# A transformer block on one core: later row passes for block 3, and an order of its own for the first attention quad

## The chip, the cores and the metric

The kernel runs on one core of a Trainium2 chip. The metric is the device time of one execution in microseconds (us). Beside the times there is a profile of one execution, with every instruction of the engines: TensorE (PE for matmuls, PEld for weight loads), VectorE (DVE), ScalarE (ACT), GpSimd (POOL) and SyncE (SP, which issues the DMAs).

## What is computed

A block with adaptive layer norms, 2048 rows of 576 values, 32 heads of 18 channels that share one key and one value head, and an MLP with 4608 hidden channels. All values are fp32.

```
mod = silu(c) @ w_mod                         # six rows: sa, ca, ga, sb, cb, gb
h = layernorm(x) * (1 + ca) + sa
q = h @ wq;  k = h @ wk;  v = h @ wv          # 32 heads of q, one k, one v
p = softmax(q k^T * 18**-0.5)
x = x + ga * ((p v) @ wo)
h = layernorm(x) * (1 + cb) + sb
x = x + gb * (gelu(layernorm(h) @ w1 + b1) @ w2 + b2)
```

## The kernel before

**The first part: projections.** The 2048 rows are four blocks (tb = 0 to 3) of 512. For each block the normalized rows are turned (channels on partitions) into a tile zt of five chunks of channels, k = 0 to 4. Each chunk is kept as a rounded part and a remainder, so that products keep their precision. `h_evac` makes a chunk: ScalarE applies scale and shift into a buffer hf (three buffers, L249); the rounded part zt[k] is a copy of hf, by ScalarE (L253) or, where `first` is set, by VectorE (L251); the remainder zt[KD+k] is hf minus the rounded part, by the engine `e` (L254).

For blocks 1 and 2 `h_chunk` turns the rows by matmuls with an identity. Block 3's rows are turned by VectorE and two trips through memory instead: they are stored to hscr and loaded back by `h_load` (L211, L213), which is issued in block 2's second step (i = 1), and `h_chunk` takes the loaded rows.

`q_chunk` projects one chunk m of queries (and, in m = 4, keys and values): 14 matmuls (L272), three for each k up to 3 and two for k = 4, into one of three psB banks; ScalarE evacuates it twice (qf L302, qs L303), GpSimd subtracts (L304), and SP stores it to qscr. In every block the steps i = 0 to 4 take m = 4, 0, 1, 2, 3. Between a chunk's matmuls `mid` puts parts of the row maxima of the first quads: one part is two pairs of matmuls (L343), each into one of two psA tiles, and two reductions on VectorE (L368). In block 2 there is one part in each step, and two in the last one. In block 3 larger units (`smax_half`, L361) follow.

While block 2 is projected, `h_chunk` for block 3 is called in the steps i = 2 (k = 0 to 2) and i = 3 (k = 3 and 4), behind `q_chunk` of the same step. The order of the calls is the order of each engine's queue: the schedule is written by hand.

**The attention.** 32 quads of four heads by 512 rows follow. The order of work of a quad is a list of tokens: S0, S1 a score matmul on one half of the array's rows (L987, into one of four psB banks), which ScalarE turns into exponentials in P (L989); M0, M1 a matmul for a row maximum of a coming quad (L343, one of three psM banks), reduced by VectorE (L1009); X1 and R1 two steps of a shorter way to a maximum (X: L997, ScalarE L1000; R: L343, VectorE L1007); Vn the product with the values for n quarters of a chunk of 128 keys (L977), which lags eight quarters behind; F1 and F2 finish the maxima of the next quad and put them into its query tile by four DMAs (L388); the others are steps of the quad before, which do nothing in the first quad. In quad 0, each M token while 3 to 7 quarters have been counted is preceded by one matmul whose result isn't used (L1064). QUAD is the list of the quads 0 to 8, QUADW of 9 to 30, LAST of 31.

The rest (output projection, second layer norm, MLP) is not touched.

Of the kernel before, what the change touches and what calls it, by code (L numbers as in the profile page):

```python
# [15 lines left out]
NB = 4  # L16
TB = S // NB
NT = TB // 128
KD = 5
NQ = H // 4  # L20
# [12 lines left out]
def block_kernel(ctx: ExitStack, tc, x, wqkv, wo, w1, b1, w2, b2, c, wmod, ident_in, out):  # L33
    nc = tc.nc
    ve, ac, po, pe, sy = nc.vector, nc.scalar, nc.gpsimd, nc.tensor, nc.sync
# [17 lines left out]
    def psB(): return PS["t"].tile([128, 512], F32, name="psB", bufs=PS["b"])  # L53
# [3 lines left out]
    def big(): return per.tile([128, 10, 512], F32R, name="big", bufs=3)  # L57
# [99 lines left out]
    def tr(o, Z, k):  # L157
        pe.transpose(o, Z[:, 128 * k:128 * (k + 1)], ident)
# [45 lines left out]
    def h_rows(tb):  # L204

        return Zs[tb].rearrange("p t c -> p (t c)").rearrange("p (k n) -> p k n", n=TB)
# [39 lines left out]
    def h_evac(p, zt, k, e, first=False):  # L246

        hf = p1.tile([128, TB], F32, name="hf", bufs=3)
        ac.activation(hf, p, AF.Identity, scale=mcol[:, 1, k:k + 1], bias=mcol[:, 0, k:k + 1])  # L249
        if first:  # L250
            ve.tensor_copy(zt[:, k, :], hf)  # L251
        else:
            ac.activation(zt[:, k, :], hf, AF.Copy)  # L253
        e.tensor_tensor(zt[:, KD + k, :], hf, zt[:, k, :].bitcast(F32), op=ALU.subtract)  # L254

    def h_chunk(tb, zt, k):
        if tb == NB - 1:
            p = h_rows(tb)[:, k]
        else:
            p = psB()  # L260
            for t in range(NT):
                tr(p[:, 128 * t:128 * (t + 1)], Zs[tb][:, t, :], k)
        h_evac(p, zt, k, ve if tb == 1 and k in (1, 3, 4) else po, tb == 1 and k < 3)

    def proj(o, wh, wl, c0, c1, zt, mid=None, n=0):
        terms = []
# [27 lines left out]
    def q_chunk(tb, m, zt, mid, n):  # L294

        w = 126 if m < KD - 1 else 128
        wd = 126 if m < KD - 1 else 72
        pq = psB()
        proj(pq[:w], wqh, wql, 126 * m, 126 * m + w, zt, mid, n)
        qs = p1.tile([128, 2, TB], F32R, name="qs", bufs=2)  # L300
        qf = p1.tile([128, TB], F32, name="qf", bufs=2)
        ac.activation(qf[:w], pq[:w], AF.Copy)  # L302
        ac.activation(qs[:w, 0], pq[:w], AF.Copy)  # L303
        po.tensor_tensor(qs[:w, 1], qf[:w], qs[:w, 0].bitcast(F32), op=ALU.subtract)  # L304
        if m == KD - 1:
            if tb >= 2:
                key_diff(tb, qf)
        sy.dma_start(qscr[tb, :, 126 * m:126 * m + wd, :].rearrange("s p t -> p s t"), qs[:wd].bitcast(F32))
        return qf, qs

    def k_block(tb, qs):

        pk = psB()
        for i in range(2):
            pe.matmul(pk, pick[:, i, :], qs[:, i, :], start=(i == 0), stop=(i == 1))
        ac.activation(KS[:, TB * tb:TB * (tb + 1)], pk, AF.Identity, bias=ones)

    def v_block(tb, qf):
        pk = psB()
        for i in range(NT):  # L320
            pe.transpose(pk[:, 128 * i:128 * (i + 1)], qf[:, 128 * i:128 * (i + 1)], ident)
        ve.tensor_copy(V[:, NT * tb:NT * (tb + 1), :DH],
                       pk.rearrange("p (i c) -> p i c", i=NT)[:, :, 72:72 + DH])
# [80 lines left out]
    zt = big()  # L404
# [22 lines left out]
    def dense(n, w, x):  # L427

        p = psB()
        for _ in range(n):  # L430
            pe.matmul(p, w, x, start=True, stop=True)
# [36 lines left out]
    def unit():  # L468
        nonlocal u1
        smax_half(1, u1 % 2, u1 // 2)  # L470
        u1 += 1
# [5 lines left out]
    for tb in range(NB):  # L477
        nz = big() if tb + 1 < NB else None
        for i, m in enumerate((4, 0, 1, 2, 3)):
            np_ = NPART[tb][i]  # L480
            if i == 2:
                parts.extend((u, tb) for u in range(8))
            mid = {(NB - 1, 1): unit, (NB - 1, 4): lambda: last.popleft()()}.get((tb, i), part)
            qf, qs = q_chunk(tb, m, zt, mid, np_ + 1 if np_ else 0)
            if i == 0:
                qv = qf, qs
            if i == 1:
                k_block(tb, qv[1])
                v_block(tb, qv[0])
                if tb == 0:  # L490
                    load_q(0)
            if i == 2:
                if tb == 0:
                    load_q(1)
            if tb == NB - 1:
                if i == 0:
                    unit()
                elif i == 3:
                    smax_fin1(0)
                if i == 4:  # L500
                    dense(5, wqh[:, 0, :128], KS[:, :512])
                    unit()
                    dense(4, wqh[:, 0, :128], KS[:, :512])
            if nz is not None:
                if tb == NB - 2 and i == 1:
                    h_load(tb + 1)
                for k in {1 + tb // 2: (0, 1, 2), 2 + tb // 2: (3, 4)}.get(i, ()) if tb else {3: (0, 1, 2), 4: (3, 4)}.get(i, ()):
                    h_chunk(tb + 1, nz, k)
            if tb < 2:
                for _ in range(NAPPLY[tb][i]):  # L510
                    b, t = applies.popleft()
                    ln1_apply(b, t, ve if b == 1 and t % 2 else ac)
                for _ in range(NSTAT[tb][i]):
                    ln1_stats(*stats.popleft())
        zt = nz
# [262 lines left out]
    def wo_add(tb, t, h2, p):  # L778
        X = XT[:, NT * tb + t, 288 * h2:288 * (h2 + 1)]
        ve.tensor_tensor(X, p[:, :288], X, op=ALU.add)  # L780
# [143 lines left out]
    def tail_parts(o, tail, d, e=po):  # L924

        e.tensor_tensor(d, tail[:, 0], tail[:, 1], op=ALU.subtract)
        for x, y in ((o[:, :2], tail), (o[:, 2], d)):
# [11 lines left out]
    QUAD = """S0 M0 S1 S1 M0 V3 S0 M1 S1 M0 M1 S0 V3 M0 S1 M1 S0 V2 M0 S1 S1 M0 X1 S0 V4 T1 X1 M0 M1 M0 S1 S0  # L939
            V4 S1 RC M0 S1 S0 M0 S0 M1 V3 S0 M1 R1 S1 S0 M0 X1 V3 M0 S1 S1 R1 S0 M0 S1 V3 M0 X1 M0 S0 S1 S0  # L940
            M1 V3 M0 S1 S1 M0 S0 R1 S0 V3 R1 S0 S1 M1 S0 M0 X1 V3 M0 S1 M0 S1 S0 S0 R1 V3 M0 X1 S0 M1 S0 M1
            V3 S1 M0 M0 S1 T2 S0 S1 V4 M0 S1 S0 M1 S0 M1 V3 S0 R1 S1 M0 F1 S1 S0 V3 X1 M0 S1 M0 R1 S0 F2 OS
            V4 M0 M1 S0 S1 M0 X1 V4 S1 M0 S1 S0 M1 M0 S1 V2 R1 S0 M1 S0 V2 S0 S1 M0 M1 V2 S1""".split()
    QUADW = """M1 M1 S0 S0 X1 S1 M0 V4 S1 M0 S1 S0 M1 M0 V4 M0 S1 S0 M0 S1 T1 M0 X1 V4 S1 RC S0 S0 M1 M0 S1 V4
            S0 R1 M1 S0 S1 M0 S1 V3 S1 M0 S0 X1 M0 M0 S1 V2 M0 S1 S0 R1 V2 M0 X1 M0 S1 S0 S1 M0 V4 S0 T2 R1
            M0 S1 OS S0 M1 WO S0 R1 M1 S0 M1 S0 X1 V3 S0 M1 M0 S1 S1 M1 S0 V3 M0 S1 S0 R1 S0 M0 X1 V3 M0 S1
# [91 lines left out]
    for n in range(NQT):  # L1038
        ns = [0, 0]
        if n < NQT - 1:  # L1040
            order = QUADW if n > NQ else QUAD
        else:
            order = LAST
        if n < NQT - 1:
            kf, kr = (sum(int(tok[1]) for tok in order[:order.index(a)] if tok[0] == "V") // 4 for a in ("F2", "RC"))
            quiet = kf - 2, kf - 1, kr - 1
        for tok in order:
            if tok[0] == "V":
                g = int(tok[1:])
                while g:  # L1050
                    i = min(g, 4 - pq % 4)
                    if pq >= LAG:
                        pv_mm(*divmod((pq - LAG) // 4, 16), pq % 4, pq % 4 + i)
                    pq, g = pq + i, g - i
                    if pq % 4 == 0:
                        between(*divmod(pq // 4 - 1, 16))
            elif tok[0] == "S":
                g = int(tok[1])
                two = sum(ns) % 7 % 2 if n == NQT - 1 else ns[g] % 2 and n == NQT - 2 and ns[g] > 24
                st_mm(n, ns[g] // 2, g, ns[g] % 2, psM if two else psB)  # L1060
                ns[g] += 1
            elif tok in maxima:
                if n == 0 and 3 <= pq < LAG and tok[0] == "M":
                    pe.matmul(idle, KS[:64, :128], KS[:64, :512], start=True, stop=True)  # L1064
                unit = next(maxima[tok], None)
                if unit:
                    mx_mm(*unit, tok[0], int(tok[1]))
            elif tok == "WO":
                wo_next(psB)
            elif tok == "WP":  # L1070
                h2 = part.popleft()
                p = psB()
                wo_mm(NB - 1, 2, h2, p, 0, KD - 1, KD - 1)
                wo_add(NB - 1, 2, h2, p)
            elif tok == "RW":
                for i, w in enumerate("hl"):
                    sy.dma_start(WO[w][:, KD - 1, :].bitcast(F32), woscr[i])
            elif tok[0] == "F":
                (smax_fin1 if tok == "F1" else smax_fin2)(n + 1)
            elif n:  # L1080
                if next(posts[0], 0) == 0:
                    posts.pop()
        if n == NQT - 1:
            W1["r"] = per.tile([128, 40, 128], F32R, name="w1a", tag="big", bufs=3)
            load_w1(0, " ".join(OPS) + " tails")
# [482 lines left out]
```

## Time and profile before

| what | value |
|---|---|
| median of 3 runs | 2213.87 us (2212.64 to 2214.05) |
| profiled execution | 2212.6 us |
| its span, first to last instruction | 2210.3 us |
| projections (first part) | to about 128 us |
| first quad | about 128 to 166 us |

The profile's span leaves out what lies ahead of the first and behind the last instruction. Times in the rows are counted from the span's start. In a timeline a row is one or more instructions of a line (xcount) that follow one another; its first two numbers are the start and the time to the end of the last one, and in brackets stands how long the engine was idle before and what ended that.

### The profile page before, as it was taken

The page shows a single profiled execution, that of the slowest core. Times are in us where ns is not written, and L with a number is a line of the kernel's source. Part 1 is how long each engine was busy: PE and PEld are TensorE (multiplying, and loading weights), DVE is VectorE, ACT ScalarE, POOL GpSimd, SP SyncE. Part 2 cuts the span into 40 slices and gives each one's busy share as a digit, 9 for nine tenths or more (in the row PEclk, how much of TensorE's full clock was granted, in tenths as well). Part 3 has the DMA queues.
Part 4 walks back from the last instruction along what each step waited for, and adds up shares of the span by engine and source line. Part 5 has one row for each costly group of instructions (what it writes and reads, how often), then busy time and mean ns, then how long its engine had stood idle before and what let it go on. Part 6 is the DMA issues. An engine that isn't in the chain of part 4 may idle for free.

```text
span 2210.3 us, 46102 instructions
## 1 busy us (share of the span) xinstructions
PE 2189.5 (99%) x16554; PEld 1439.5 (65%) x16554; DVE 1938.3 (88%) x3425; ACT 1624.8 (74%) x3110; POOL 1521.7 (69%) x1760
## 2 busy tenths in 40 slices
PE   8999999999999999999999999999999999999999
PEld 6655444444544545444454445899898899889898
DVE  7689999999999999999999993888888878787887
ACT  5579999999999999999999998544445444343443
POOL 7654456666777678678675640888899767877776
PEclk9999999999999999999999999999999999999999
DMA  6432143433443442343343321666767746676664
GB/s 231 131 133 93 35 134 118 136 130 113 136 130 125 127 141 98 126 139 117 123 131 121 125 71 59 204 194 190 203 185 199 207 133 179 184 218 188 178 184 124
DMA packets 243688, 320.16 MB, mean 145 GB/s; under 512 B 67871, under 2 KB 133807, under 8 KB 243461
## 3 DMA queue, kind: packets, MB, share of 16 engines
q1 hardware_dynamic: 243317, 317.08, 47.0%
q8 instruction: 131, 2.15, 0.4%
q14 instruction: 96, 0.79, 0.1%
q10 hardware_dynamic: 144, 0.15, 0.0%
HBM read 207.23 MB, written 99.69 MB: 139 GB/s over the span
## 4 chain that ended last, share of the span: by engine, by line
PE 95%; DVE 2%; ACT 1%; POOL 1%; issue 1%; DMA 1%; SPq 0%; ACTq 0%; POOLq 0%; DVEq 0%
PE psC L977 24%; PE psB L1204 18%; PE psA L1307 16%; PE psB L987 14%; PE psM L343 13%; PE psB L776 2%; PE psB L997 2%; PE psA L1341 1%; PE psB L272 1%; PE psA L776 1%; PE psA L343 0%; DMA Z<-hscr 0%; DVE mx L368 0%; PE psB L381 0%; PE psM L987 0%
## 5 line engine op out<-in xcount | busy, mean ns | idle before, releaser
L989 ACT ACTIVATE P<-psB 128x512 f32<-128x512 f32 x2013 | 1054.9, 620 | 48.7 <-PE psM L343 26.9
L1009 DVE TENSOR_REDUCE mx<-psM 128x1 f32<-128x512 f32 x1476 | 931.2, 682 | 26.0 <-PE psM L343 11.0
L987 PE MATMUL psB<-qst,KS 64*128 64x512 f32 x2013 | 604.2, 433 | 0.1
L343 PE MATMUL psM<-KS,qst 64*128 64x512 f32 x1722 | 592.5, 434 | 0.4 <-DVE mx L361 0.3
L977 PE MATMUL psC<-P,V 128*32 128x256 f32 (+3 forms) x6608 | 568.1, 439 | 0.0
L987 PEld LDWEIGHTS psB<-qst,KS 64*128 64x128 f32 x2013 | 301.9, 184 | 216.2 <-ACT P L989 184.7
L343 PEld LDWEIGHTS psM<-KS,qst 64*128 64x128 f32 x1722 | 285.1, 184 | 188.4 <-DVE mx L1009 139.4
L1204 PE MATMUL psB<-ops,w1a 128*128 128x512 f32 x1512 | 393.8, 396 | 0.2 <-DVE h L1219 0.2
L1204 PEld LDWEIGHTS psB<-ops,w1a 128*128 128x128 f32 x1512 | 270.1, 188 | 46.8 <-DVE h L1219 0.6
L977 PEld LDWEIGHTS psC<-P,V 128*32 128x32 f32 x6608 | 147.0, 108 | 187.9 <-issue 160.1
L1313 DVE TENSOR_TENSOR XT<-psA,XT 128x576 f32<-128x576 f32 x330 | 241.5, 752 | 16.2 <-PE psA L1307 10.7
L1307 PEld LDWEIGHTS psA<-w2s,big 128*128 128x128 f32 x1584 | 223.7, 188 | 12.2 <-DVE XT L1313 0.2
L1307 PE MATMUL psA<-w2s,big 128*128 128x288 f32 x1584 | 230.2, 294 | 0.0
L1281 POOL TENSOR_TENSOR big<-s,big 128x512 fp32r<-128x512 f32 x132 | 171.1, 1296 | 10.6
L1007 DVE CUSTOM_DVE_ANT_0 xc<-psM,xc 128x512 f32<-128x512 f32 x246 | 165.9, 681 | 11.2 <-PE psB L987 5.7
L1217 ACT ACTIVATE psB<-gs 128x512 f32<-128x512 f32 x144 | 86.7, 602 | 120.8 <-DVE gs L1216 120.8
L1213 ACT ACTIVATE h<-psB,b1t 128x512 f32<-128x512 f32 x144 | 98.1, 681 | 105.2 <-PE psB L1204 98.7
L1000 ACT ACTIVATE xc<-psB 128x512 f32<-128x512 f32 x246 | 153.8, 625 | 3.9 <-PE psB L987 1.2
L813 POOL TENSOR_TENSOR os<-O,os 128x512 fp32r<-128x512 f32 x31 | 39.9, 1287 | 169.1 <-ACT os L812 169.1
L1216 DVE SCALAR_TENSOR_TENSOR gs<-psB,h 128x512 f32<-128x512 f32 x144 | 98.9, 687 | 38.8 <-ACT psB L1214 38.7
L847 POOL TENSOR_TENSOR r<-r,r 128x256 fp32r<-128x256 f32 (+1 forms) x162 | 122.0, 753 | 13.0
L1222 ACT ACTIVATE big<-h 128x512 fp32r<-128x512 f32 x39 | 24.7, 634 | 139.3 <-DVE h L1219 139.3
(219 smaller groups left out, 3290.4 us busy)
## 6 DMA issues: line engine op xcount, KB each, us to landing
w1a<-w1scr SPq DMA_DIRECT2D x252, 256.0 KB
w2s<-w2sum SPq DMA_DIRECT2D x132, 288.0 KB
w1scr<-r SPq DMA_DIRECT2D x126, 256.0 KB
w2s<-w2scr SPq DMA_DIRECT2D x76, 288.0 KB
w2scr<-r SPq DMA_DIRECT2D x72, 288.0 KB
w2sum<-r SPq DMA_DIRECT2D x72, 288.0 KB
qst<-qscr SPq DMA_DIRECT2D x192, 72.0 KB
w1a<-w2scr SPq DMA_DIRECT2D x33, 288.0 KB
```

The source lines that it names most:

```text
L343: pe.matmul(o, QST[n][64 * g:64 * g + 64, p, 128 * qt:128 * (qt + 1)], KS[64 * g:64 * g + 64, 512 * kb:512 * (kb + 1)], start=True, stop=True)
L847: po.tensor_tensor(o[:, n:2 * n], src, o[:, :n].bitcast(F32), op=ALU.subtract)
L977: pe.matmul(PVt[n][32 * j:32 * (j + 1), cs], V[:, kc, :], t[:, j, cs], start=(kc == 0 and h0 == 0), stop=(kc == 15), skip_group_check=True)
L987: pe.matmul(t, KS[64 * g:64 * g + 64, 128 * kc:128 * (kc + 1)], QST[n][64 * g:64 * g + 64, i, :], start=True, stop=True)
L989: ac.activation(P[n, kc][:, 2 * i + g, :], t, AF.Exp, scale=SCALE)
L1000: ac.activation(XC[-1], t, AF.Relu)
L1007: ve.tensor_tensor_reduce(c, t, c, 1.0, -3.0e38, ALU.add, ALU.max, o)
L1009: ve.tensor_reduce(o, t, axis=AX.X, op=ALU.max)
L1204: pe.matmul(o, x, y, start=(first and i == 0), stop=(i == len(terms) - 1), skip_group_check=True)
L1281: po.tensor_tensor(unit(u, 1), x, unit(u, 0).bitcast(F32), op=ALU.subtract)
L1307: pe.matmul(p[:, i, :288], x[:, ts_], W2S[k][:, y], start=(bool(first) and q == 0), stop=(q == 2), skip_group_check=True)
L1313: ve.tensor_tensor(o, p[:, :, :288], o, op=ALU.add)
```

## The change

Three edits. The remainders of block 3's chunks 1 and 3 are subtracted on VectorE instead of GpSimd, and the rounded parts of its chunks 0 to 2 are copied on VectorE instead of ScalarE. All five chunks of block 3 are made in step i = 3 of block 2, behind the projection of m = 2; before, three were made in step 2 and two in step 3. Quad 0 gets a list of its own, QUAD0, with 19 V tokens where QUAD has 21, and F1 and F2 later in the list; the counts of S, M, X and R are the same.

```diff
-        h_evac(p, zt, k, ve if tb == 1 and k in (1, 3, 4) else po, tb == 1 and k < 3)
+        on_ve = {1: (1, 3, 4), NB - 1: (1, 3)}.get(tb, ())
+        h_evac(p, zt, k, ve if k in on_ve else po, tb in (1, NB - 1) and k < 3)
...
-                for k in {1 + tb // 2: (0, 1, 2), 2 + tb // 2: (3, 4)}.get(i, ()) if tb else {3: (0, 1, 2), 4: (3, 4)}.get(i, ()):
+                for k in ({3: (0, 1, 2), 4: (3, 4)}, {1: (0, 1, 2), 2: (3, 4)}, {3: range(KD)})[tb].get(i, ()):
                     h_chunk(tb + 1, nz, k)
...
+    QUAD0 = """S1 S0 M1 S0 V4 M0 S1 M0 S1 S0 M1 V4 S1 M0 T1 M1 S0 S1 S0 M1 V4 X1 M0 R1 S0 X1 M0 S0 V3 S1 M0 S1 S0
+            M1 M0 S1 V3 M1 S0 S1 M0 X1 M0 S1 V3 M0 S1 M0 S1 S0 M1 V3 M0 S1 S0 S0 R1 M1 S0 V3 S1 M0 S0 S1 R1 S1
+            M0 V3 M0 X1 S0 S1 M1 M0 S1 V3 M1 S0 RC S0 X1 R1 M0 S1 V3 S1 M0 S0 R1 S0 M0 S1 V4 S0 M1 S0 X1 M0 X1
+            M0 V4 M0 S1 M0 R1 S0 S1 S0 V4 X1 M0 S0 R1 S1 M0 V3 M0 S1 S0 S1 M1 S0 V4 F1 M0 S1 M0 M1 S0 S1 F2 V3
+            S0 R1 S0 S1 M1 S1 M0 V3 M0 T2 S1 S1 S0 M0 OS M1 S0 V3 S0 M1 M0""".split()
...
-            order = QUADW if n > NQ else QUAD
+            order = QUADW if n > NQ else QUAD if n else QUAD0
```

For comparison, QUAD begins and ends so:

```
S0 M0 S1 S1 M0 V3 S0 M1 S1 M0 M1 S0 V3 M0 S1 M1 S0 V2 M0 S1 S1 M0 X1 S0 V4 T1 X1 M0 M1 M0 S1 S0 V4 ...
... S0 R1 S1 M0 F1 S1 S0 V3 X1 M0 S1 M0 R1 S0 F2 OS V4 M0 M1 S0 S1 M0 X1 V4 S1 M0 S1 S0 M1 M0 S1 V2
R1 S0 M1 S0 V2 S0 S1 M0 M1 V2 S1
```

## Rows read from the trace of the kernel before

**Rows 1.** The page, part 1: busy time, share of the span, instructions.
```profile
PE 2189.5 (99%) x16554; PEld 1439.5 (65%) x16554; DVE 1938.3 (88%) x3425; ACT 1624.8 (74%) x3110; POOL 1521.7 (69%) x1760
```
**Rows 2.** Windows: length, busy time by engine, granted clock, DMA.
```profile
93.00:102.90 9.90, 8.07 (x33) 4.04 (x31) 5.70 (x5) 8.77 (x16) 8.74 (x7) 1.00 0.17 56
```
**Rows 3.** Timeline of ScalarE around block 3's rows.
```profile
92.45 0.81 ACT L249 ACTIVATE hf<-Z,mcol 128x512 f32<-128x512 f32 x1 [5.27 <-DMA Z<-hscr]
...
96.58 0.58 ACT L302 ACTIVATE qf<-psB 126x512 f32<-126x512 f32 x1
```
**Rows 4.** Timeline of TensorE, block 2's last steps and block 3's first.
```profile
84.08 3.53 PE L272 MATMUL psB<-big,wA 128*126 128x512 f32 x14
...
91.18 0.73 PE L343 MATMUL psA<-KS,qst 64*128 64x512 f32 x4
...
93.19 0.50 PE L343 MATMUL psA<-KS,qst 64*128 64x512 f32 x2
94.13 0.49 PE L343 MATMUL psA<-KS,qst 64*128 64x512 f32 x2 [0.44 <-DVE mx L368]
94.55 3.13 PE L272 MATMUL psB<-big,wA 128*126 128x512 f32 x11
...
102.89 1.89 PE L272 MATMUL psB<-big,wA 128*126 128x512 f32 x7
```
**Rows 5.** Waits from 84 to 103.5 us: total, times, longest.
```profile
PE psB L272 <- POOL big L254: 1.3, 2, 1.0
...
PEld psA L343 <- ACT qs L303: 0.4, 1, 0.4
```
**Rows 6.** Timeline of VectorE in block 2's last step.
```profile
91.72 4.62 DVE L368 TENSOR_REDUCE mx<-psA 128x2 f32<-128x1024 f32 x4 [1.28 <-PE psA L343]
```
**Rows 7.** The tile hf: durations in ns (min/median/max), first and last start.
```profile
L253 ACT ACTIVATE big<-hf x14: 631/634/637, 20.3 to 99.8; 128x512 fp32r<-128x512 f32 x14
L254 POOL TENSOR_TENSOR big<-hf,big x12: 1262/1288/1301, 45.0 to 100.5; 128x512 fp32r<-128x512 f32 x12
...
L251 DVE CAST big<-hf x6: 372/424/427, 19.6 to 42.3; 128x512 fp32r<-128x512 f32 x6
L249 ACT ACTIVATE hf<-Z,mcol x5: 799/802/817, 92.4 to 98.9; 128x512 f32<-128x512 f32 x5
```
**Rows 8.** Timeline of all engines, block 1's projection.
```profile
47.75 0.69 DVE L254 TENSOR_TENSOR big<-hf,big 128x512 fp32r<-128x512 f32 x1 [3.14 <-ACT big L253]
...
47.86 0.74 PE L343 MATMUL psA<-KS,qst 64*128 64x512 f32 x4
...
49.70 1.21 DVE L368 TENSOR_REDUCE mx<-psA 128x2 f32<-128x1024 f32 x1
```
**Rows 9.** Groups by line and shape, 24 to 29 us: count, busy, mean ns.
```profile
L415 POOL TENSOR_TENSOR wA<-bigw,wA 128x504 fp32r<-128x504 f32 x2 | 3.4, 1695 | 4.5 <-issue 4.5
...
L415 DVE TENSOR_TENSOR wA<-bigw,wA 128x504 fp32r<-128x504 f32 x1 | 1.3, 1306 | 0.4 <-ACT wA L413 0.4
```
**Rows 10.** Windows near the start: busy time by engine, granted clock, DMA.
```profile
15.00:18.50 3.50, 2.89 (x29) 2.58 (x27) 2.88 (x6) 1.62 (x6) 1.98 (x3) 1.00 1.06 374
19.00:22.00 3.00, 3.00 (x15) 2.90 (x14) 2.19 (x4) 2.97 (x5) 0.65 (x2) 0.50 1.05 391
```
**Rows 11.** Window of the first quad.
```profile
128.00:166.00 38.00, 37.57 (x344) 19.14 (x345) 36.30 (x69) 35.95 (x72) 27.44 (x16) 1.00 0.42 144
```
**Rows 12.** Timeline of ScalarE, first quad's start.
```profile
128.66 5.37 ACT L989 ACTIVATE P<-psB 128x512 f32<-128x512 f32 x10 [2.46 <-PE psB L987]
```
**Rows 13.** Timeline of TensorE in the first quad.
```profile
133.63 1.07 PE L977 MATMUL psC<-P,V 128*32 128x512 f32 x8
...
138.76 0.40 PE L987 MATMUL psB<-qst,KS 64*128 64x512 f32 x1
...
139.00 0.39 PE L987 MATMUL psB<-qst,KS 64*128 64x512 f32 x1
```
**Rows 14.** Timeline of SyncE, first quad's end.
```profile
159.66 2.85 SPq L388 DMA_DIRECT2D qst<-ms  x4
```

## The prediction

> **What bounds the kernel now.** I read the page first: TensorE is busy 99% of the span [rows 1], so the kernel gains only where TensorE waits, and loses where it is made to. The change touches two places: block 3's rows in the projections (80 to 103 us) and the first attention quad (128 to 166 us). So the windows came next, then the timelines of these places engine by engine, and the waits.
>
> In the first place TensorE is busy 8.07 of 9.90 us, ScalarE and GpSimd nearly throughout [rows 2]. ScalarE stands 5.27 us until the loaded rows arrive, at 92.45, and evacuates chunk m=2 of block 2 only at 96.58, since the row passes are ahead of it in its queue [rows 3]. On TensorE the reader should find the two maxima parts of chunk m=3. Call them B (91.18) and C (93.19, its second tile at 94.13 after 0.44 us for VectorE). Then the last four matmuls of m=3 run on into block 3's chunk m=4 (94.55), and chunk m=0 begins at 102.89 [rows 4]. Within that stretch TensorE waits 1.3 us by name for GpSimd's subtractions [rows 5]. VectorE reduces B and C in one go of four from 91.72, with 1.28 us of idleness ahead [rows 6].
>
> **The row passes: what they remove and add.** Five 0.80 us passes on ScalarE stay; three of its 0.63 us roundings become VectorE copies of 0.42, and two of the five GpSimd subtractions of 1.29 [rows 7] become VectorE subtractions of 0.69 [rows 8]. All five chunks now follow m=2's evacuation. That frees m=2's PSUM bank some 6 us earlier, but little waits for it: three banks rotate, and the one wait that names ScalarE's qs is 0.4 us of a weight load [rows 5]. No DMA moves: the load is issued where it was, so the rows still arrive at 92.45; the store of m=2 goes out earlier, behind that arrival.
>
> What costs is the queue of VectorE. It gets the new copies and subtractions ahead of B's and C's reductions, because m=3 is issued after them. psA has two tiles; B fills both, so C cannot start before B is reduced. Does VectorE keep the program's order? In block 1, whose evacuation has the same mix, it sat 3.14 us for a rounding at 47.75, and only at 49.70 reduced a tile whose matmuls began at 47.86 [rows 8]: the next subtraction stands between. I take it that it does.
>
> The chain [rows 7, 8]: the first pass ends at 92.45+0.80 = 93.25; the copy takes it to 93.7; GpSimd's subtraction to 95.0. There are three hf buffers, so the fourth pass (k=3) waits for this subtraction: 95.0 to 95.85, its rounding on ScalarE to 96.5, its subtraction on VectorE to 97.2. Copies and subtraction of k=1 and 2 fit in between. Only then can B be reduced. (The fifth chunk has nothing on VectorE; its subtraction on GpSimd ends at about 99.5, ahead of its use.)
>
> Two of VectorE's subtractions now meet one on GpSimd. Near the start there is such a meeting: 1.31 us on VectorE where 0.69 is usual, and 1.70 on GpSimd where 1.29 is [rows 9]. The bounds are 0 and (1.31-0.69)+(1.70-1.29) = 1.0 us on the chain; the meetings overlap only in part, so I take 0.6, and B's reductions start at 97.8. The Trainium skill (GPSIMD Engine Reference, section Specifications) says that the two engines share their SBUF interfaces, and counts VectorE's two-port operations as well as those with two SBUF inputs. By that rule the new copies too would slow GpSimd, an estimate of 0.2 us more; no row here shows it.
>
> Each reduction takes 4.62/4 = 1.16 us [rows 6]. C's first tile can start at 97.8+1.2 = 99.0, its second at 100.2 against 94.13 now: 6.1 us late. TensorE stands from about 93.2 to 99.0, then but for two matmuls to 100.2. Part of it comes back. From 94.55 to 102.89 there are 8.34 us, in which 18 projection matmuls at 0.25 (fourteen take 3.53) and two maxima parts of about 0.7 are 5.9 us of work [rows 4]; the other 2.4 us are waits for the row passes and go, as all passes are done before. In their place the unit after m=4 waits some 0.5 us for VectorE, which is still two reductions behind. Net: 6.1-2.4+0.5 = **+4.2 us**, bounds 3.5 (no meeting) to 4.6 (full). Everything behind follows TensorE's order, so I see no slack that takes this back.
>
> **The clock.** The granted clock was 1.00 from 15.0 to 18.5, while TensorE did only small matmuls with waits between, and 0.50, its 1.2 GHz level, from 19 to 22 [rows 10]. A stand of nearly 6 us is emptier than that stretch. By the rows alone a fall is one occurrence; I give it seven in ten. Its price: at the lower level matmuls last twice as long. If the level is back up before C is through, only C's matmuls are longer, about 0.2 us. If it lasts into the dense stretch behind, 5 us of it at half rate lose 2.5. I take **1.3 us**, the middle. The Trainium skill (TensorE: Matmul & The Clock Gate, section HAM oscillation) says that waits between bursts of matmuls put the array back to its lower clock, a rule that speaks against the change. By it every run would pay, and rival (a) below would drop out.
>
> **The first quad.** It takes 38.0 us, with ScalarE busy 35.95 and VectorE 36.30 [rows 11]. The counts are the same in both orders (64 S, 48 M, 8 X, 8 R), so it can't get much below these two. The old order has 11 S, one X and 9 M before the first V that does work, which starts at 133.63 [rows 13]. Four psB tiles allow the twelfth evacuated tile only after the eighth evacuation: 128.66+8x0.53 = 132.9 [rows 12]. In the new order 10 S and 7 M stand ahead, so the tenth waits for the sixth, 131.9, and the first V comes about 1.3 us earlier. One S, one X and two M are left for later, and some stand worse for running on both row halves at once: by the tokens 62 slots behind the first V against 58, a slot being 0.24 us (138.76 to 139.00) [rows 13], so 1.0 us more. That leaves 0.3. One working V token fewer helps a little, and ScalarE and VectorE, already within 1.7 to 2.1 us of the quad's length, may bring a wait. I take **-0.3 us**, bounds -1.4 (38.0 less the 36.3, and 0.3 for the start) and +1 (two evacuations' worth of waits).
>
> The filling matmuls of the start go from 5 to 3; they stand where TensorE waits for evacuations anyway. F2 comes about 2 us nearer to the quad's end. Its four DMAs keep SP 2.85 us from 159.66 [rows 14], with a quad end near 166; two microseconds later the last is issued about 1.5 us ahead of the S that reads it, so a short wait is possible there, which the +1 covers.
>
> **Sum.** Without the clock: 4.2-0.3 = +3.9. With it: +5.2. Against the profiled execution's 2212.6 us that is 2217.8; the median of the runs shown is 1.3 us above that execution, so I forecast 2213.9+5.2 = 2219.1. A measurement of this kernel tells about 0.2%, 4.4 us, from no change; the forecast lies just beyond.
>
> **Rivals.** (a) *Held, but the clock stays up*: 2217.8, within the bound. For it: one fall is on record in this trace. Against it: TensorE never stands so long elsewhere in the projections. (b) *Not slower: VectorE reduces B as soon as it is ready*, at 91.7, ahead of the row passes. Then C starts at 94.1 as now, the copies slip in between reductions, the 1.3 us of waits go [rows 5], and with -0.3 the time is 2212.3. It decides if C's second tile starts before 95; the order in block 1 speaks against it [rows 8]. (c) *The new order of the first quad costs*: ScalarE or VectorE run dry, or F2's rows land late. At +1 instead of -0.3, on top of hold and clock: 2220.4. For it: the 1.5 us above; against it: equal counts.
>
> **Chances.** Held with the fall 0.58, (a) 0.24, (b) 0.06, (c) 0.12. Of the first some three quarters lie beyond 4.4 us (the clock's price must exceed 0.5), of (a) a fifth (full meeting, nothing from the quad), of (c) nearly three quarters: slower 0.57, within 0.40, faster 0.03, the last from (b) with more waits gone than I found. The range goes from 2214.5, which leaves (b) out, to 2221.5, hold and fall with the upper half of the clock's price and of (c).
>
> **What would show it.** Right: a gap on TensorE from about 93 to C's first tile at 98.5 to 99.5, released by VectorE's mx; on VectorE copies from 93.3 and a subtraction that ends at 97 to 98; a granted clock of 0.50 somewhere in 96 to 105; chunk m=0 of block 3 at 106.5 to 109 instead of 102.89; from ScalarE's first P to the first working V 3.7 us instead of 5.0; the first quad 0 to 1 us shorter, later quads as long as now. Wrong: rows that arrive before 90, C before 95, or a first quad above 38 us.

## The result, and the profile after

The changed kernel takes 2219.25 us (median of 8 runs, 2218.38 to 2221.19), the kernel before 2213.21 us beside it (8 runs): a ratio of 1.0028, 95% interval 1.0017 to 1.0038, or 6.0 us more. The profiled execution took 2219.56 us with a span of 2217.5 us. Of all the executions timed for this document one stands out, 5708 us for the kernel with the gap filled (below), for which the record gives no cause; the median of its eleven hardly feels it. In the changed kernel the line numbers are higher by 1 in the first part and by 6 in the attention.

TensorE's timeline, from part B of chunk m=3 to block 3's chunk m=0 (110.36):

```profile
91.79 0.73 PE L344 MATMUL psA<-KS,qst 64*128 64x512 f32 x4
...
100.08 0.79 PE L344 MATMUL psA<-KS,qst 64*128 64x512 f32 x2 [6.21 <-DVE mx L369]
101.21 0.80 PE L344 MATMUL psA<-KS,qst 64*128 64x512 f32 x2 [0.34 <-DVE mx L369]
101.94 4.88 PE L273 MATMUL psB<-big,wA 128*126 128x512 f32 x11
106.75 0.73 PE L344 MATMUL psA<-KS,qst 64*128 64x512 f32 x4
...
110.36 1.89 PE L273 MATMUL psB<-big,wA 128*126 128x512 f32 x7
```

Part B stands 0.6 us later than before [rows 4]; that is ahead of the change and not part of it (in the kernel with only the first quad's order, below, whose rows are those of before, B stands at 92.05). Counted from B, chunk m=0 came 11.71 us later before and comes 18.57 us later now: 6.9 us are lost here. The loss starts at one place, 6.21 us in which TensorE waits for VectorE's mx, where it waited 0.44 us [rows 4]. What follows is slow too: eleven matmuls take 4.88 us where they took 3.13, waits included.

VectorE's timeline over the same stretch:

```profile
93.88 0.43 DVE L251 CAST big<-hf 128x512 fp32r<-128x512 f32 x1 [2.84 <-ACT hf L249]
94.58 1.35 DVE L251 CAST big<-hf 128x512 fp32r<-128x512 f32 x1 [0.28 <-ACT hf L249]
95.97 0.69 DVE L254 TENSOR_TENSOR big<-hf,big 128x512 fp32r<-128x512 f32 x1
96.58 0.42 DVE L251 CAST big<-hf 128x512 fp32r<-128x512 f32 x1
97.20 1.69 DVE L254 TENSOR_TENSOR big<-hf,big 128x512 fp32r<-128x512 f32 x1 [0.20 <-ACT big L253]
98.81 4.60 DVE L369 TENSOR_REDUCE mx<-psA 128x2 f32<-128x1024 f32 x4
```

VectorE was idle for 2.84 us up to 93.88, the last 1.5 of them with the first tile of part B ready (about 92.3); but the copy of k=0 was next in its queue and waited for ScalarE's first pass. Two of the five row operations are long, the copy of k=1 (1.35 us, others 0.42) and the subtraction of k=3 (1.69, the other 0.69). ScalarE and GpSimd show what they met:

```profile
93.03 2.23 ACT L249 ACTIVATE hf<-Z,mcol 128x512 f32<-128x512 f32 x3 [1.15 <-DMA Z<-hscr]
95.69 0.82 ACT L249 ACTIVATE hf<-Z,mcol 128x512 f32<-128x512 f32 x1 [0.43 <-POOL big L254]
```
```profile
94.39 1.27 POOL L254 TENSOR_TENSOR big<-hf,big 128x512 fp32r<-128x512 f32 x1 [1.09 <-DVE big L251]
97.07 1.27 POOL L254 TENSOR_TENSOR big<-hf,big 128x512 fp32r<-128x512 f32 x1 [1.42 <-DVE big L251]
98.61 1.40 POOL L254 TENSOR_TENSOR big<-hf,big 128x512 fp32r<-128x512 f32 x1 [0.27 <-ACT big L253]
```

Each long operation began while a GpSimd subtraction was running (94.58 behind 94.39, 97.20 behind 97.07), and that subtraction itself kept its 1.27 us. The windows (length, busy time of PE, PEld, DVE, ACT, POOL, granted clock, DMA) show why TensorE is slow behind the gap:

```profile
93.00:96.00 3.00, 0.87 (x4) 0.38 (x2) 1.81 (x3) 2.54 (x4) 1.56 (x2) 1.00 0.57 198
96.00:98.00 2.00, 0.00 (x0) 0.00 (x0) 1.80 (x3) 1.94 (x4) 0.93 (x1) 0.56 0.01 3
98.00:100.00 2.00, 0.00 (x0) 0.00 (x0) 2.00 (x3) 0.53 (x1) 1.73 (x2) 0.50 0.00 0
...
102.00:104.00 2.00, 2.00 (x6) 1.63 (x6) 1.42 (x2) 0.00 (x0) 0.00 (x0) 0.50 0.00 0
104.00:107.00 3.00, 3.00 (x10) 2.06 (x10) 0.00 (x0) 1.08 (x2) 1.27 (x1) 0.59 0.00 0
```

The granted clock falls to 0.50 inside the gap and is back only near the end of the last window.

The first quad, after, in TensorE's and ScalarE's timelines: the first score matmul, the first working V, a broadcast that stands behind the last V (L560), and ScalarE's evacuation of the finished quad during the next one (L792).

```profile
135.35 0.50 PE L993 MATMUL psB<-qst,KS 64*128 64x512 f32 x2
...
139.65 1.06 PE L983 MATMUL psC<-P,V 128*32 128x512 f32 x8
...
171.75 0.43 PE L560 MATMUL psB<-bigw,unity 128*32 128x144 f32 x8
```
```profile
177.97 0.61 ACT L792 ACTIVATE O<-psC 128x512 f32<-128x512 f32 x1
```

The same four marks before, the first V being that of [rows 13]:

```profile
128.13 0.61 PE L987 MATMUL psB<-qst,KS 64*128 64x512 f32 x2
...
165.32 0.43 PE L559 MATMUL psB<-bigw,unity 128*32 128x144 f32 x8
```
```profile
170.95 0.61 ACT L791 ACTIVATE O<-psC 128x512 f32<-128x512 f32 x1
```

From the first score matmul they come after 5.50 (133.63), 37.19 and 42.82 us before, after 4.30, 36.40 and 42.62 us now: 1.2 us is won at the first V, 0.8 is left behind the last V, and 0.2 when the next quad evacuates.

### The profile page after: what moved, and what is told of

It is laid out like the page before. It is cut to its first block, busy times and chain, and to the rows that moved or that the text cites. A ratio compares the mean times of both kernels' runs of the same rounds, so it can differ in the third digit from the quotient of the medians.

```text
span 2217.5 us, 46084 instructions
## 1 busy us (share of the span) xinstructions
PE 2192.7 (99%) x16544; PEld 1440.8 (65%) x16544; DVE 1942.1 (88%) x3430; ACT 1622.8 (73%) x3107; POOL 1517.6 (68%) x1758
## 4 chain that ended last, share of the span: by engine, by line
PE 95%; DVE 2%; ACT 1%; POOL 1%; DMA 1%; issue 1%; SPq 0%; ACTq 0%; POOLq 0%; DVEq 0%
PE psC L983 24%; PE psB L1210 18%; PE psA L1313 16%; PE psB L993 14%; PE psM L344 13%; PE psB L777 2%; PE psB L273 2%; PE psB L1003 2%; PE psA L1347 1%; PE psA L777 1%; PE psA L344 1%; DVE mx L369 0%; DMA Z<-hscr 0%; PE psB L382 0%; PE psM L993 0%
```

## The experiments

The theory after the result: (1) VectorE, in the order of its queue, holds parts B and C behind the row operations; (2) the empty gap lets the clock fall, which costs some 2 us more; (3) the first quad's order gives something back. The rivals are named with each run. All times are medians beside runs of the kernel before on the same chip: 2213.45 us for the first four kernels, 2213.51 for the others.

**Only the rows' edit.** The first quad goes by QUAD again.

```diff
-            order = QUADW if n > NQ else QUAD if n else QUAD0
+            order = QUADW if n > NQ else QUAD
```

> Only the edit of block 3's rows; the first quad keeps its old order. Theory (the rows cost some 6.9 us, a hold of 4.5 and a clock price of 2.4, and the new first quad gives back 0.8): 2220.0 us, chunk m=0 of block 3 7 us later than before, the first quad 38 us as before. Rival (the first quad's order is worth nothing, or what it gains is lost in the next quads): 2219.2 us, the same as with both edits.

Measured: 2220.23 us, ratio 1.0030 (1.0019 to 1.0042). The whole loss is the rows'. The time is at the theory's value, but the intervals don't part it from the changed kernel; the marks of its first quad do: 37.13 us to the broadcast and 42.78 to the evacuation, as before the change.

**Only the first quad's order.** QUAD0 in the kernel before.

```diff
+    QUAD0 = """S1 S0 M1 S0 V4 M0 S1 ...""".split()
-            order = QUADW if n > NQ else QUAD
+            order = QUADW if n > NQ else QUAD if n else QUAD0
```

> Only the new order of the first quad; block 3's rows as before. Theory: 2212.4 us, 0.8 less than before (2213.2), first working V 4.3 us after the first S instead of 5.5, no wait for F2's rows. Rival (the gain is lost in the next quads): 2213.2 us; rival (the order costs when it isn't started late): 2214 us or more.

Measured: 2213.36 us, ratio 0.9999 (0.9990 to 1.0008). The interval holds the theory's 2212.4 as well as the first rival's 2213.2, so the time doesn't decide; the marks do. Here too the first V comes early (133.15 after 128.84) and the broadcast after 36.41 us, but the evacuation only after 42.64, where the kernel before has 42.82. So the theory's 0.8 us, read at the broadcast behind the last V, shrinks to 0.2 in the next quad: by the marks the rival holds.

**The gap filled.** TensorE works through most of the gap.

```diff
+    def filled_part():
+        seen.append(0)
+        if len(seen) == 2:
+            dense(24, wqh[:, 0, :128], KS[:, :512])
+        part()
...
-            mid = {(NB - 1, 1): unit, (NB - 1, 4): lambda: last.popleft()()}.get((tb, i), part)
+            mid = {(NB - 1, 1): unit, (NB - 1, 4): lambda: last.popleft()(), (2, 4): filled_part}.get((tb, i), part)
```

> The changed kernel, with 24 matmuls whose result isn't used on TensorE between the second five matmuls of m=3 and part C, so that the gap stays and TensorE works in it. Theory (the clock falls for the empty gap and costs 2.4 us): granted clock 1.00 from 94 to 107, C at the same time as in the changed kernel, 2216.8 us. Rival (the hold on VectorE is all, what runs slower on TensorE is hidden behind it): clock 1.00 but 2219.2 us.

Measured: 2217.99 us, ratio 1.0022 (1.0012 to 1.0031). The clock column of the windows stays at 1.00:

```profile
98.00:100.00 2.00, 1.57 (x7) 0.94 (x5) 2.00 (x2) 0.87 (x2) 1.75 (x2) 1.00 0.00 0
100.00:102.00 2.00, 0.91 (x4) 0.37 (x4) 2.00 (x3) 0.00 (x0) 0.40 (x1) 1.00 0.00 0
102.00:104.00 2.00, 2.00 (x11) 1.63 (x10) 1.80 (x2) 0.74 (x2) 0.00 (x0) 1.00 0.00 0
```
```profile
91.89 0.73 PE L344 MATMUL psA<-KS,qst 64*128 64x512 f32 x4
...
93.82 5.75 PE L432 MATMUL psB<-KS,wA 128*128 128x512 f32 x24
100.46 0.50 PE L344 MATMUL psA<-KS,qst 64*128 64x512 f32 x2 [0.90 <-DVE mx L369]
101.60 0.50 PE L344 MATMUL psA<-KS,qst 64*128 64x512 f32 x2 [0.63 <-DVE mx L369]
102.02 2.82 PE L273 MATMUL psB<-big,wA 128*126 128x512 f32 x11
...
108.39 1.89 PE L273 MATMUL psB<-big,wA 128*126 128x512 f32 x7
```
```profile
93.36 2.23 ACT L249 ACTIVATE hf<-Z,mcol 128x512 f32<-128x512 f32 x3 [1.37 <-DMA Z<-hscr]
```

The reader is to see that C still waits for VectorE, at the same place, while the eleven matmuls behind it take 2.82 us instead of 4.88. From C's second tile to m=0 are 6.79 us here (101.60 to 108.39) and 9.15 in the changed kernel (101.21 to 110.36). So the lower clock costs 2.36 us by the rows, 2.05 behind the start of the eleven matmuls and 0.3 in C's second tile; the theory had 2.4. By the medians it is 1.5 us (4.5 above the kernel before, against 6.0), and 2.2 beside the kernel with only the rows' edit, timed in the same round. The interval of this run holds the theory's time as well as the rival's, so it is the rows that decide.

What is left, the hold alone, is 4.5 us: 6.9 lost between B and m=0 in the changed kernel, less 2.36. Counted in this run itself it is 16.50-11.71 = 4.8, but here C came 0.3 us later behind B (8.57 us after it, 8.29 in the changed kernel), mostly because the loaded rows did: the first pass starts 1.47 us behind B, 1.24 in the changed kernel. Over the runs in which the passes wait for the rows and B has its old place this arrival lies 1.0 to 1.7 us behind B, and the hold goes with it, so one profile gives the hold to some tenths of a us.

**No row operation on VectorE.** The move to the later step stays.

```diff
-        on_ve = {1: (1, 3, 4), NB - 1: (1, 3)}.get(tb, ())
-        h_evac(p, zt, k, ve if k in on_ve else po, tb in (1, NB - 1) and k < 3)
+        on_ve = {1: (1, 3, 4)}.get(tb, ())
+        h_evac(p, zt, k, ve if k in on_ve else po, tb == 1 and k < 3)
```

> The changed kernel with block 3's copies on ScalarE and all its subtractions on GpSimd again: only the move to the later step and the first quad's order are left. Theory (the copies and subtractions on VectorE hold part C): no gap, C's second tile at about 94.1 to 94.7, TensorE waits at most 1.3 us for the last subtractions, clock 1.00, 2211.4 to 2212.4 us. Rival (passes made one step later are late for chunk m=4, whichever engine makes them): TensorE waits 3 us or more at m=4, 2215 us or more.

Measured: 2211.63 us, ratio 0.9991 (0.9982 to 1.0000), as the theory had it and below the rival's time.

```profile
94.30 0.49 PE L344 MATMUL psA<-KS,qst 64*128 64x512 f32 x2 [0.44 <-DVE mx L369]
94.72 2.84 PE L273 MATMUL psB<-big,wA 128*126 128x512 f32 x11
...
99.33 0.97 PE L273 MATMUL psB<-big,wA 128*128 128x512 f32 x3 [0.21 <-POOL big L254]
100.69 0.49 PE L273 MATMUL psB<-big,wA 128*128 128x512 f32 x1 [0.40 <-POOL big L254]
...
101.78 1.89 PE L273 MATMUL psB<-big,wA 128*126 128x512 f32 x7
```

C starts as in the kernel before, and TensorE's named waits for GpSimd shrink from 1.3 us [rows 5] to 0.6. From B (91.34) to m=0 are 10.44 us, 1.3 less than before, so by the rows the move to the later step is good by itself. This is the fastest kernel of the study, 1.8 us under the kernel before, and its interval just reaches no change; beside the kernel with only the first quad's order, which it differs from by the move alone, it is 1.7 us faster.

**The subtraction of k=3 on GpSimd.**

```diff
-        on_ve = {1: (1, 3, 4), NB - 1: (1, 3)}.get(tb, ())
+        on_ve = {1: (1, 3, 4), NB - 1: (1,)}.get(tb, ())
```

> The changed kernel with the subtraction of k=3 on GpSimd again. Theory (B is held until VectorE's last operation for the rows): that is now the copy of k=2, some 1.8 us sooner than the subtraction of k=3, so part C starts 1.8 us sooner and the hold is 2.7 us instead of 4.5; with a clock price of 0 to 2 us 2216 to 2218 us, against 2219.5 for the changed kernel on this scale (before 2213.4). Rival (the hold comes from the loaded rows or ScalarE's passes, not from VectorE's last operation): 2219.5 us.

Measured: 2217.73 us, ratio 1.0019 (1.0010 to 1.0028). On VectorE the reductions follow the copy of k=2 at once:

```profile
96.82 0.42 DVE L251 CAST big<-hf 128x512 fp32r<-128x512 f32 x1
97.15 4.61 DVE L369 TENSOR_REDUCE mx<-psA 128x2 f32<-128x1024 f32 x4
```

TensorE's gap shrinks from 6.21 to 4.34 us. The clock falls in this one too (0.50 from 98 to 104). The last row operation on VectorE sets the hold.

**The parts moved ahead.**

```diff
-    NPART = ((0, 0, 0, 0, 0), (1, 1, 1, 1, 1), (1, 1, 1, 1, 2), (1, 1, 2, 2, 2))
+    NPART = ((0, 0, 0, 0, 0), (1, 1, 1, 1, 1), (1, 1, 2, 2, 0), (1, 1, 2, 2, 2))
```

> The changed kernel with the maxima parts of block 2 moved forward: two in m=1, two in m=2, none in m=3, so that no part stands behind the row passes in VectorE's queue until block 3's m=4. Theory (only a part that stands behind the passes and needs a tile is held): no gap in m=3, clock 1.00, VectorE still makes the copies and two subtractions; TensorE waits 0.4 us twice for a tile in m=1 and m=2; 2211.8 us. Rival (VectorE makes the row chunks so late that m=4 waits for them): a wait of 2 us or more in m=4, 2214 us or more.

Measured: 2213.56 us, ratio 1.0000 (0.9991 to 1.0009). The gap is gone and the clock stays at 1.00, so the hold needs a part behind the row operations. But the time is 1.8 us above the expectation, which lies just inside the interval. ScalarE and TensorE show a part of it:

```profile
94.34 0.60 ACT L303 ACTIVATE qf<-psB 126x512 f32<-126x512 f32 x1 [4.56 <-PE psB L273]
...
95.31 2.23 ACT L249 ACTIVATE hf<-Z,mcol 128x512 f32<-128x512 f32 x3
```
```profile
98.65 1.64 PE L273 MATMUL psB<-big,wA 128*128 128x512 f32 x6 [0.92 <-POOL big L254]
...
102.90 0.50 PE L273 MATMUL psB<-big,wA 128*128 128x512 f32 x1 [0.34 <-POOL big L254]
```

With two parts in it m=2 ends later, and the row passes stand behind its evacuation on ScalarE: they begin at 95.31 instead of 93.03 in the changed kernel. That is the rival's case in a small size, passes too late for m=4: TensorE waits 1.3 us for them, as in the kernel before [rows 5], not the 2 or more that the rival asks for. What makes up the rest of the 1.8 us was not followed.

**All subtractions on VectorE.**

```diff
-        on_ve = {1: (1, 3, 4), NB - 1: (1, 3)}.get(tb, ())
+        on_ve = {1: (1, 3, 4), NB - 1: (0, 1, 2, 3, 4)}.get(tb, ())
```

> The changed kernel with all five subtractions of block 3's chunks on VectorE, none on GpSimd. Theory (VectorE's copies and subtractions were long because a GpSimd subtraction ran beside them): every copy takes 0.42 to 0.43 and every subtraction 0.69 to 0.70 us, part B is held until the subtraction of k=4, about as long as in the changed kernel; 2219 to 2220 us. Rival (they are long because hf was just written, or for waits of their own): one copy of 1.3 us or a subtraction of 1.7 remains, B is held 1 us or more longer than in the changed kernel, 2220.5 us or more.

Measured: 2218.82 us, ratio 1.0024 (1.0014 to 1.0033). With GpSimd idle, every operation has its short duration:

```profile
94.61 0.69 DVE L254 TENSOR_TENSOR big<-hf,big 128x512 fp32r<-128x512 f32 x1
95.22 0.42 DVE L251 CAST big<-hf 128x512 fp32r<-128x512 f32 x1
...
98.30 0.69 DVE L254 TENSOR_TENSOR big<-hf,big 128x512 fp32r<-128x512 f32 x1 [0.27 <-ACT big L253]
98.91 4.61 DVE L369 TENSOR_REDUCE mx<-psA 128x2 f32<-128x1024 f32 x4
```

So the long ones were long for GpSimd's work beside them, and the hold, now until k=4, is as long as with two subtractions: C's first tile comes 8.36 us behind B, 8.29 in the changed kernel.

**The engines without the move.**

```diff
-                for k in (..., {3: range(KD)})[tb].get(i, ()):
+                for k in (..., {2: (0, 1, 2), 3: (3, 4)})[tb].get(i, ()):
```

> The changed kernel without the move: block 3's chunks in steps 2 and 3 as before, but with the copies and two subtractions on VectorE. Theory (the queue of VectorE holds the next part): it is now part A of m=2 that stands behind the passes, so TensorE waits at part B from about 91 to 97 and once more at C; a hold of 5 us, and the clock falls: 2219 to 2221 us. Rival (the cost comes from moving the passes to the later step): no long gap, 2214 us or less.

Measured: 2219.54 us, ratio 1.0026 (1.0016 to 1.0036). The gap has moved forward by one chunk, to part B:

```profile
97.88 0.79 PE L344 MATMUL psA<-KS,qst 64*128 64x512 f32 x2 [6.08 <-DVE mx L369]
```
```profile
93.58 0.43 DVE L251 CAST big<-hf 128x512 fp32r<-128x512 f32 x1 [6.70 <-ACT hf L249]
...
96.61 2.35 DVE L369 TENSOR_REDUCE mx<-psA 128x2 f32<-128x1024 f32 x2
98.87 0.95 DVE L254 TENSOR_TENSOR big<-hf,big 128x512 fp32r<-128x512 f32 x1
```
```profile
98.01 1.27 POOL L305 TENSOR_TENSOR qs<-qf,qs 126x512 fp32r<-126x512 f32 x1
99.23 1.73 POOL L254 TENSOR_TENSOR big<-hf,big 128x512 fp32r<-128x512 f32 x1
```

VectorE waits 6.70 us for the first pass, with part A's reductions behind the copy in its queue. The second wait, at C, that the theory expected didn't come. The engines cost, with or without the move; the rival falls. (The last three lines are taken up at the end.)

## Why the prediction came out as it did

The forecast was 2219.1 us; the way there held, with one term, the price of the clock, much too small. That it lies 0.15 us from the measured median is in part luck: its base, 2213.9 us from three runs, was 0.7 above the median beside the changed kernel. The change itself was forecast as +5.2 us and measured as +6.0. Its times below are set against the changed kernel's less the 0.6 us that part B stood later.

| step | predicted | after |
|---|---|---|
| the rows arrive, first pass | 92.45 | 92.4 |
| fourth pass, behind GpSimd's first subtraction | 95.0 | 95.1 |
| B's reductions | 97.8 | 98.2 |
| C's first and second tile | 99.0, 100.2 | 99.5, 100.6 |
| from m=3's last matmuls to m=0, clock at 1.00 | 6.4 us | 6.37 us (gap filled) |
| hold in all, at full clock | +4.2 | +4.5 counted from B |
| price of the clock | +1.3 | +2.36 |
| first quad | -0.3 | -0.2 |

Of its signs, VectorE's last subtraction (97 to 98 foretold) ended at 98.3 on this scale and m=0 (106.5 to 109) stood at 109.8, both a little beyond; the others came as foretold.

- *VectorE keeps the program's order and holds B and C.* Shown: without its row operations the gap is gone, with fewer it is shorter, without the move it goes one part ahead, without parts behind them there is none. Rival (b), that B is reduced as soon as it is ready, is out.
- *The hold, +4.2.* Right to 0.3 us. C's second tile came 6.5 us late (6.1 predicted), and 2.0 came back at full clock (8.76 us from it to m=0 before, 6.79 with the gap filled; 1.9 predicted). The difference lies in the meetings of VectorE and GpSimd. The prediction let two subtractions of VectorE meet GpSimd, both engines pay, and put 0.6 us on the chain. In the run one subtraction and one copy of VectorE began inside a GpSimd subtraction, VectorE alone paid in both, and the subtraction that ends the chain took 1.69 us, 1.0 more than usual, the upper bound. The Trainium skill (GPSIMD Engine Reference, section Specifications) counts VectorE's two-port operations among those that meet GpSimd; if the copy of k=1 is one of them, which no run here shows, its 1.35 us agree. But GpSimd was not slowed by it: it kept 1.27 us, and of the 0.2 us that the prediction had estimated from that rule nothing was seen.
- *The clock.* It fell in all five kernels in which TensorE stood empty for B's reductions, for 4.34 to 6.66 us: 0.50 was granted from 98 to 106 us with only the rows' edit and with all subtractions on VectorE, from 98 to 104 with that of k=3 on GpSimd, from 96 to 102 without the move. It stayed at 1.00 in the filled one. Rival (a) is out. The Trainium skill (TensorE: Matmul & The Clock Gate, section HAM oscillation) says that waits between bursts of matmuls put the array back to its lower clock; these five agree. The price was mis-sized: 2.36 us against the 1.3 taken between 0.2 and 2.5. Of the prediction's two cases it was the second, since the lower level lasted through nearly all of the eleven matmuls behind C.
- *The first quad, -0.3.* Right in size, and at its start for the reason given: the first V came 1.2 us earlier (1.3 predicted). Nearly all of it was lost again, 0.4 by the last V and 0.6 in the next quad; that the slots left for later took it, as the prediction has it, no run shows. Alone it is no change that can be measured. F2's rows made no wait that the trace names; rival (c) didn't come.
- *What comes back.* Some 0.25 us of the loss returned between m=0 and the first quad (24.99 us from one to the other after, 25.24 before), which the prediction had not seen.

The sum of the measured terms, 4.5+2.36-0.25-0.2 = 6.4 us, stands against 6.6 between the two spans (2217.5 less 2210.3, less 0.6) and 6.0 between the medians.

## What to carry to other kernels

Before work is moved to an engine with idle time, ask what stands behind it in that engine's queue: here VectorE was idle when it got the copies, but they wait for a late load, and everything behind them waits as well. Cost a stall of TensorE with what the granted clock takes behind it: 2.4 us on top of 4.5 here. And read the gain of a reordered list at a mark behind which nothing of it is left: the first quad's order won 1.2 us at its start, 0.8 at its last V, and 0.2 in the next quad.

## What the runs showed of the hardware that was not expected

When VectorE and GpSimd met in row operations between SBUF tiles, one of them was longer and the other was not. In the changed kernel it was VectorE: a copy of 128x512 took 1.35 us instead of 0.42, a subtraction 1.69 instead of 0.69, while GpSimd's subtraction kept 1.27 us. GpSimd's next one took 1.40, and in the kernel without the move one took 1.73. In each of these meetings the one that began second paid, by about what was left of the other, less some 0.15 us: VectorE's subtraction at 97.20 had 1.14 us of GpSimd's ahead of it and took 1.00 longer; the copy at 94.58 had 1.08 and took 0.93 longer; GpSimd's subtraction at 98.61 had 0.28 of VectorE's and took 0.13 longer; without the move GpSimd's at 99.23 had 0.59 of VectorE's (98.87, itself longer for GpSimd's that ran until 99.28) and took 0.46 longer. Near the start of the kernel before, where both were longer [rows 9], VectorE's began at 25.15, inside the first of GpSimd's two (together 24.22 to 27.58), and the second of these inside VectorE's. All this is read from the order of the starts in the traces; no run moved a start alone to try it.

The lower clock outlasted the gap: in the changed kernel it stood at 0.50 from 98 to 104, though TensorE was busy throughout from 102, and it came back between 104 and 107.
